# Turning x by small transfers and block transposes instead of by TensorE, in a fused attention and MLP kernel

## The chip, the core and the metric

The kernel runs on one core of one Trainium2 chip. The metric is device time in microseconds, from launch to the last output. The core has five engines that run side by side and wait for one another by semaphores: TensorE (PE in the profile, with its weight loads as PEld), VectorE (DVE), ScalarE (ACT), GpSimd (POOL) and SyncE (SP, which here only issues transfers). TensorE writes to PSUM, a memory of eight banks of 128 partitions x 512 floats; everything else lies in SBUF. Instructions of one engine run in the order in which the kernel writes them.

## What is computed

The reference, cut to what matters:

```
phi(x)[i,j] = (S1 x)[i] * (S2 x)[j]          # 8 x 8 = 64 features of a 32-wide row
kv  = sum over s of phi(k)[s] (x) v[s]       # 64 x 32 for each batch and head
z   = sum over s of phi(k)[s]                # 64
num = phi(q) kv ;  den = phi(q) z + 1e-6     # for each token and head
x   = num / den, the 4 heads side by side    # 4 x 1088 tokens, 128 wide
out = x + relu(layernorm(x) * g @ w1) @ w2   # 128 -> 512 -> 128
```

There are 4 batches, 4 heads, 1088 tokens and a head width of 32; all data are float32.

## The kernel before, in words

**Chunks.** The 4352 tokens are cut into nine chunks. Chunks 0 to 7 are 512 tokens each, two to a batch (four tiles of 128 tokens); chunk 8 (`LAST`) collects the last 64 tokens of all four batches in two tiles. For a chunk c these stages follow one another:

- `query_rows(c)` (L316): DVE turns the chunk's q by 32x32 blocks (L233; L325 for chunk 8), so that the head dimension lies on partitions.
- `query_features(c)` (L329): 32 matmuls (L340) put both factors of the features into banks 0 to 3. ACT copies one factor to SBUF (L348) and DVE multiplies the other one, straight from the banks, with it (L349, tile `qp`).
- `numerators(c)` (L354): 64 small matmuls (L370) of the features with `kvz`, the batch's kv and z, into banks 0 and 1. DVE takes the denominators (L377), inverts them (L382) and writes x = num / den (L384): tokens on partitions, 128 columns to a tile.
- `statistics(c)` (L394): DVE takes mean and variance of each tile (L401), and six small POOL instructions finish the variance.
- `root(c)` (L418): ACT takes the root (L422), DVE the reciprocal (L426), and four POOL instructions (L427 to L432) refine it to `rstd`.
- `turn_x(c)` (L434): TensorE transposes the tiles of x into bank 7 (L440) and ACT copies them to SBUF (L442, tile `xT`), so that the 128 columns of x lie on partitions.
- `hidden(c, j)` for j of 0 to 3 (L444): w1 times `xT` into bank 4 or 5 in turn (L449), then relu on ACT (L452, tile `hT`). Mean and scale are folded in: the mean into w1, `rstd` into the end.
- `second(c)` (L458): 16 matmuls with w2 into bank 6 (L462); `result(c)` (L467): DVE adds x to `rstd` times the bank (L473), and SP issues four transfers of 32 rows each to the output (L483).

**Keys.** A batch's keys need `key_rows` (DVE, L233 and L246), `key_tokens` (copies of v), `key_features(b, part, at)` (TensorE, L266, and an ACT copy, L271), `key_products` (POOL, L282) and `key_values(b, at, t0, t1)` (TensorE, L299), which sums kv and z over nine tiles of tokens in one bank, here bank 3, and copies them out by ACT (L307, L309). Batch 0 and the preparation of w1 and w2 stand ahead of the loop.

**Order.** The order on every engine is written out by hand (`manual_schedule`, and the loop at L552). In iteration c the loop issues the hidden layer of chunk c, `root(c)`, the numerators of chunk c + 1, in odd iterations the features and products of a coming batch's keys, the statistics of c + 1, `second(c)`, `turn_x(c + 1)`, `query_rows(c + 2)`, `result(c)` and `query_features(c + 2)`. In iterations 2 and 4 `key_values` runs in two halves, one inside the hidden layer (ahead of j = 2) and one behind `second`. In iteration 7 `turn_x(8)` stands inside `second(7)`; the hidden layer of chunk 8 follows in iteration 8.

**Transfers.** Each transfer that SP or ACT issues signals on one of eight semaphores, taken in turn, so the ninth waits for the first to have landed. The page's part on issues calls the time from issue to that signal "us to landing".

Of the kernel before, what the change touches and what calls it, by code (L numbers as in the profile page):

```python
# [15 lines left out]
def _ap(t: bass.AP, p0: int, np_: int, off: int, free):  # L16

    p = list(t.ap)[0]
    return bass.AP(
        t.tensor, t.offset + p0 * p[0] + off, [[p[0], np_]] + [list(d) for d in free]  # L20
    )
# [8 lines left out]
def kernel(  # L30
# [26 lines left out]

    nc = tc.nc  # L60
    P = 128
    B, H, S, D = q.shape
    R = S1.shape[0]
    DM = H * D
# [11 lines left out]

    consts = ctx.enter_context(tc.tile_pool(name="consts", bufs=1))
    work = ctx.enter_context(tc.tile_pool(name="work", bufs=2))
    small = ctx.enter_context(tc.tile_pool(name="small", bufs=3))
    ps = ctx.enter_context(tc.tile_pool(name="ps", bufs=1, space=bass.MemoryType.PSUM))  # L80
    ctx.enter_context(tc.manual_schedule())
    banks = ps.tile([P, 8 * 512], F32, name="banks")
# [1 line left out]
    def bank(i):  # L84
        return banks[:, 512 * i : 512 * (i + 1)]
# [225 lines left out]
                kvp[F * (1 - i) : F * (2 - i), 0 : 2 * D1],  # L311
            )

    qTs, qps, xs, rs, mvs, xTs, hTs = {}, {}, {}, {}, {}, {}, {}

    def query_rows(c):  # L316
        if c > LAST:
# [36 lines left out]
    def numerators(c):  # L354


        if c > LAST:
            return
        x = xs[c] = work.tile([P, 512], F32, tag="x", name="x", bufs=3)
        qp, n = qps.pop(c), ntiles(c) // 2  # L360
        step = 64 if c < LAST else 32
        for i in range(n):
            for h in range(H):
                for half in range(2):
                    rows = slice(F * half, F * half + F)
                    for u in range(0, P, step):
                        kvz = kvzs[CHUNKS[c][0] if c < LAST else u // 32]
                        t, o = 256 * h + P * i + u, W * i + D1 * h
                        z = D1 * (h // 2) + (0 if h % 2 == half else 2 * D1)
                        nc.tensor.matmul(  # L370
                            bank(half)[u : u + step, o : o + D1], qp[rows, t : t + step],
                            kvz[rows, z : z + D1], start=True, stop=True,
                        )
        den = small.tile([P, 4 * H], F32, tag="den", name="den")
        rden = small.tile([P, 4 * H], F32, tag="rden", name="rden")
        m = n * H
        nc.vector.tensor_scalar(  # L377
            out=_ap(den, 0, P, 0, [[m, 2], [1, m]]),
            in0=_ap(banks, 0, P, D, [[512, 2], [D1, m]]),
            scalar1=1e-6, scalar2=None, op0=ALU.add,  # L380
        )
        nc.vector.reciprocal(rden[:, 0 : 2 * m], den[:, 0 : 2 * m])  # L382
        for half in range(2):
            nc.vector.tensor_tensor(  # L384
                out=_ap(x, 0, P, D * m * half, [[D, m], [1, D]]),
                in0=_ap(banks, 0, P, 512 * half, [[D1, m], [1, D]]),
                in1=_ap(rden, 0, P, m * half, [[1, m], [0, D]]),
                op=ALU.mult,
            )

    def ntiles(c):
        return 4 if c < LAST else 2

    def statistics(c):  # L394

        if c > LAST:
            return
        n, x = ntiles(c), xs[c]
        st = small.tile([P, 4 * 6], F32, tag="st", name="st")
        for i in range(n):  # L400
            nc.vector.bn_stats(out=st[:, 6 * i : 6 * i + 6], in_=x[:, DM * i : DM * (i + 1)])  # L401
        d, s, va, r1 = (
            small.tile([P, 4], F32, tag=tag, name=tag)[:, 0:n] for tag in ("d", "s", "va", "r1")
        )

        def of(k):
            return _ap(st, 0, P, k, [[6, n]])

        tt, ts = nc.gpsimd.tensor_tensor, nc.gpsimd.tensor_scalar
        tt(out=d, in0=of(1), in1=of(4), op=ALU.subtract)  # L410
        tt(out=s, in0=of(2), in1=of(5), op=ALU.add)
        tt(out=d, in0=d, in1=d, op=ALU.mult)
        ts(out=s, in0=s, scalar1=1.0 / DM, scalar2=1e-6, op0=ALU.mult, op1=ALU.add)
        ts(out=d, in0=d, scalar1=0.25, scalar2=None, op0=ALU.mult)
        tt(out=va, in0=d, in1=s, op=ALU.add)
        mvs[c] = va, r1

    def root(c):  # L418

        n = ntiles(c)  # L420
        va, r1 = mvs.pop(c)
        nc.scalar.activation(r1, va, AF.Sqrt)  # L422
        r0 = small.tile([P, 4], F32, tag="r0", name="r0")[:, 0:n]
        rs[c] = small.tile([P, 4], F32, tag="rstd", name="rstd")
        tt = nc.gpsimd.tensor_tensor
        nc.vector.reciprocal(r0, r1)  # L426
        tt(out=r1, in0=va, in1=r0, op=ALU.mult)  # L427
        tt(out=r1, in0=r1, in1=r0, op=ALU.mult)
        nc.gpsimd.tensor_scalar(
            out=r1, in0=r1, scalar1=-0.5, scalar2=1.5, op0=ALU.mult, op1=ALU.add  # L430
        )
        tt(out=rs[c][:, 0:n], in0=r0, in1=r1, op=ALU.mult)  # L432

    def turn_x(c):  # L434
        if c > LAST:
            return
        n, x = ntiles(c), xs[c]
        xp = bank(7)
        for i in range(n):
            nc.tensor.transpose(xp[:, P * i : P * i + P], x[:, DM * i : DM * (i + 1)], ident)  # L440
        xT = xTs[c] = work.tile([P, 512], F32, tag="xT", name="xT")
        nc.scalar.copy(xT[:, 0 : P * n], xp[:, 0 : P * n])  # L442

    def hidden(c, j):  # L444
        n = P * ntiles(c)
# [7 lines left out]

    def second_at(c, i):

        return bank(6)[:, DM * i : DM * (i + 1)] if c < LAST else bank(6 + i)[:, 0:DM]

    def second(c, i0=0, i1=4):  # L458
        hT = hTs[c]
# [7 lines left out]
    def result(c):  # L467
        n = ntiles(c)
        ob = work.tile([P, 512], F32, tag="ob", name="ob", bufs=3)
        x, rstd = xs.pop(c), rs.pop(c)  # L470
        for i in range(n):
            t = slice(DM * i, DM * (i + 1))
            nc.vector.scalar_tensor_tensor(  # L473
                out=ob[:, t], in0=second_at(c, i), scalar=rstd[:, i : i + 1], in1=x[:, t],
                op0=ALU.mult, op1=ALU.add,
            )
        by_p0, by_part = steps(CHUNKS[c][0])
        for p0 in range(4):
            if c < LAST:
                row, eng = CHUNKS[c][0] * S + by_part * CHUNKS[c][1] + by_p0 * p0, nc.sync  # L480
            else:
                row, eng = p0 * S + 32, (nc.sync, nc.scalar)[p0 % 2]
            eng.dma_start(  # L483
                out=bass.AP(out.tensor, out.offset + row * DM, [[G * DM, 32], [1, n * DM]]),
                in_=ob[32 * p0 : 32 * p0 + 32, 0 : n * DM],
            )
# [5 lines left out]
    def first_weight(i):  # L492

        w1p, terms = bank((4, 7)[i]), w1_terms[i]
        for j, term in enumerate(terms):
            nc.tensor.matmul(  # L496
                w1p[:, 0:256], center, term, start=(j == 0), stop=(j == len(terms) - 1)
            )
        nc.scalar.copy(w1[:, 256 * i : 256 * i + 256], w1p[:, 0:256])
# [49 lines left out]
        nc.gpsimd.tensor_tensor(out=w2, in0=up, in1=rest[0], op=ALU.add)  # L549


    for c in range(LAST + 1):  # L552
        b = c // 2 + 1
        even = c > 0 and c % 2 == 0 and b < B
        if c == LAST:
            root(c)
        for j in range(JC):
            if (c, j) == (0, 1):
                first_weight(1)
            if j == 2 and even:  # L560
                key_values(b, 3, 0, 5)
            hidden(c, j)
        if c == 0:
            query_features(1)
            for part in range(3):
                key_features(1, part, (4, 7, 5)[part])
                key_products(1, part, nc.gpsimd)
            for part in range(3):
                key_tokens(1, part, nc.scalar)
            numerators(1)  # L570
            statistics(0)
            root(0)
            second(0)
            key_values(1, 3, 0, NT)
        else:
            if c < LAST:
                root(c)
            numerators(c + 1)
        if c % 2 == 1 and b + 1 < B:
            for part in range(3):  # L580
                key_features(b + 1, part, 2 + part % 2)
                key_products(b + 1, part, nc.gpsimd)
        statistics(c + 1)
        if c == LAST - 1:
            second(c, 0, 3)
            turn_x(LAST)
            second(c, 3, 4)
        elif c > 0:
            second(c)
        if even:  # L590
            key_values(b, 3, 5, NT)
        if c < LAST - 1:
            turn_x(c + 1)
        query_rows(c + 2)
        result(c)
        query_features(c + 2)
        if c % 2 == 0 and b + 1 < B:
            fill(b + 1)
            for part in range(3):
                key_tokens(b + 1, part, nc.gpsimd)  # L600
                key_rows(b + 1, part)


# [28 lines left out]
```

## Time and profile before

| what | value |
|---|---|
| time, median of 3 runs | 119.75 us (119.69 to 120.51) |
| span of the profiled execution | 121.6 us, mean granted clock 0.953 |
| TensorE busy | 111.2 us of the span, 91% |
| DVE, ACT, POOL busy | 59.0, 46.6, 39.1 us |
| share of TensorE in the chain that ended last | 82% |
| transposes of x (L440) | 34 matmuls, 5.9 us busy |
| copies of turned x (L442) | 9, 5.1 us on ACT |

The profiled execution took 123.42 us as a run. Its TensorE clock was granted at half rate between about 14 and 25 us of the span and at full rate afterwards, so what is read from 27 us on is read at full clock. How to read it: "busy" adds up instructions by engine; the chain of waits goes back from the last instruction to what released each step; an engine's row of digits has 40 slices of the span, in tenths.

### The profile page before, as it was taken

How to read it: one execution, taken by the hardware profiler on the slowest of the kernel's cores; microseconds unless marked ns; L12 is line 12 of the kernel's file. 1: busy time of each engine (PE TensorE's matmuls, PEld its weight loads, DVE VectorE, ACT ScalarE, POOL GpSimd, SP SyncE). 2: the span in 40 equal slices, each digit the busy share in tenths (PEclk: the TensorE clock that was granted, in tenths of full speed). 3: DMA queues.
4: the chain of work that ended last, by engine and by line, in shares of the span. 5: the costliest groups of instructions: out<-in, count | busy, mean ns of one | idle time of the engine just before them, and what ended most of it. 6: DMA issues, size and time to landing. Idle time of an engine off the chain costs nothing.

```text
span 121.6 us, 4288 instructions
## 1 busy us (share of the span) xinstructions
PE 111.2 (91%) x1833; PEld 80.3 (66%) x1833; DVE 59.0 (49%) x181; ACT 46.6 (38%) x109; POOL 39.1 (32%) x125
## 2 busy tenths in 40 slices
PE   5947877997999999999999999999999999999980
PEld 5826734536996399459845994598469549729770
DVE  1757679404644771616526825083417528414320
ACT  4145214259006740742176207403650570452420
POOL 4028000404967069402800892042014004204120
PEclk9999855599999999999999999999999999999997
DMA  2949999999402100210030003000300110030031
GB/s 63 306 102 309 325 211 314 225 304 258 146 3 65 29 5 3 52 40 5 0 86 5 0 5 85 7 0 5 86 0 5 41 45 5 3 89 5 0 86 43
DMA packets 8068, 10.24 MB, mean 84 GB/s; under 512 B 2417, under 2 KB 5617, under 8 KB 8049
## 3 DMA queue, kind: packets, MB, share of 16 engines
q1 hardware_dynamic: 7792, 9.38, 29.3%
q10 hardware_dynamic: 256, 0.59, 1.6%
q8 instruction: 14, 0.23, 0.8%
q14 instruction: 6, 0.04, 0.1%
HBM read 7.74 MB, written 2.23 MB: 82 GB/s over the span
## 4 chain that ended last, share of the span: by engine, by line
PE 82%; DMA 6%; DVE 3%; ACT 2%; SPq 2%; issue 1%; POOL 1%; ACTq 0%; POOLq 0%
PE banks L449 28%; PE banks L462 26%; PE banks L370 8%; PE banks L340 7%; PE banks L299 6%; PE banks L440 4%; DMA qn<-in_q_dram 4%; PE banks L266 2%; DMA vn<-in_v_dram 2%; PE banks L496 1%; DVE qp L349 1%; ACT xT L442 1%; SPq L105 1%; DVE x L384 1%; SPq L116 1%
## 5 line engine op out<-in xcount | busy, mean ns | idle before, releaser
L449 PE MATMUL banks<-xT,w 128*128 128x512 f32 (+1 forms) x72 | 35.1, 622 | 0.8 <-ACT xT L442 0.7
L462 PE MATMUL banks<-w,hT 128*128 128x128 f32 x272 | 32.9, 278 | 0.0
L462 PEld LDWEIGHTS banks<-w,hT 128*128 128x128 f32 x272 | 31.3, 192 | 0.4
L452 ACT ACTIVATE hT<-banks 128x512 f32<-128x512 f32 (+1 forms) x36 | 20.8, 576 | 13.4 <-PE banks L449 13.3
L449 PEld LDWEIGHTS banks<-xT,w 128*128 128x128 f32 x72 | 12.6, 200 | 16.7 <-ACT hT L452 7.1
L282 POOL TENSOR_TENSOR kp<-fs 128x1024 f32<-128x1024 f32 (+1 forms) x10 | 15.3, 1552 | 11.4 <-ACT fs L271 11.2
L349 DVE TENSOR_TENSOR qp<-banks,qb 128x512 f32<-128x512 f32 (+1 forms) x18 | 11.1, 656 | 15.0 <-ACT qb L348 15.0
L473 DVE SCALAR_TENSOR_TENSOR ob<-banks,rstd,x 128x128 f32<-128x128 f32 x34 | 9.7, 343 | 14.8 <-PE banks L462 6.9
L427 POOL TENSOR_TENSOR r<-va,r 128x4 f32<-128x4 f32 (+1 forms) x9 | 1.8, 201 | 45.0 <-DVE r L426 38.7
L370 PEld LDWEIGHTS banks<-kvz,qp 64*64 64x64 f32 (+1 forms) x576 | 9.0, 131 | 7.0 <-issue 3.8
L442 ACT COPY xT<-banks 128x512 f32<-128x512 f32 (+1 forms) x9 | 5.1, 563 | 22.0 <-PE banks L440 22.0
L370 PE MATMUL banks<-kvz,qp 64*64 64x33 f32 (+1 forms) x576 | 10.1, 219 | 1.3 <-DVE qp L349 0.9
L426 DVE RECIPROCAL r<-r 128x4 f32<-128x4 f32 (+1 forms) x9 | 1.6, 176 | 19.6 <-ACT r L422 19.6
L348 ACT COPY qb<-banks 128x512 f32<-128x512 f32 (+1 forms) x18 | 9.2, 566 | 4.1 <-PE banks L340 4.1
L299 PEld LDWEIGHTS banks<-v,kp 128*32 128x32 f32 (+3 forms) x432 | 7.7, 118 | 4.1 <-issue 3.1
L299 PE MATMUL banks<-v,kp 128*32 128x33 f32 (+3 forms) x432 | 8.6, 207 | 1.5 <-ACT qb L348 1.1
L340 PE MATMUL banks<-qT,wb 32*64 32x256 f32 (+1 forms) x144 | 6.7, 387 | 1.0 <-DVE qT L233 1.0
L401 DVE BATCH_NORM_STATS2 st<-x 128x6 f32<-128x128 f32 x34 | 7.3, 278 | 0.0
L384 DVE TENSOR_TENSOR x<-banks,rden 128x256 f32<-128x256 f32 (+1 forms) x18 | 6.5, 404 | 0.3
L440 PE MATMUL banks<-ident,x 128*128 128x128 f32 x34 | 5.9, 296 | 0.8 <-DVE sc L177 0.8
L340 PE MATMUL banks<-qT,wa 32*64 32x256 f32 (+1 forms) x144 | 6.3, 362 | 0.0
L233 DVE STREAM_TRANSPOSE qT<-qn 128x512 f32<-128x512 f32 x8 | 5.6, 699 | 1.4 <-DMA qn<-in_q_dram 1.4
(63 smaller groups left out, 91.4 us busy)
## 6 DMA issues: line engine op xcount, KB each, us to landing
out_dram<-ob SPq DMA_DIRECT2D x32, 64.0 KB, 1.7
kn<-in_k_dram SPq DMA_DIRECT2D x3, 544.0 KB, 6.1
qn<-in_q_dram SPq DMA_DIRECT2D x3, 544.0 KB, 5.6
vn<-in_v_dram SPq DMA_DIRECT2D x12, 128.0 KB, 5.9
vn<-in_v_dram SPq DMA_DIRECT2D x8, 64.0 KB, 3.2
w_raw<-in_moe_w_ch_dram ACTq DMA_DIRECT2D x1, 512.0 KB
w_raw<-in_moe_w_ch_dram SPq DMA_DIRECT2D x1, 512.0 KB
kn<-in_k_dram SPq DMA_DIRECT2D x1, 288.0 KB, 3.0
```

The lines of the kernel that those rows point to most:

```text
L282: eng.tensor_tensor(out=_ap(kp, 0, m, t0 * H * F, [[F, tiles * H], [R, R], [1, R]]), in0=_ap(kf, 0, m, 0, [[R2, tiles * H], [1, R], [0, R] ...
L299: nc.tensor.matmul(kvp[o : o + step, D1 * (h // 2) : D1 * (h // 2 + 1)], kp[0:m, H * F * t + f : H * F * t + f + step], v1[0:m, W * t + D1 ...
L340: nc.tensor.matmul(bank(h)[F * half : F * half + F, o : o + n], w[rows, :], qT[rows, n * half : n * half + n], start=True, stop=True,)
L348: nc.scalar.copy(own, _ap(banks, 0, P, 512 * h, [[512, 2], [1, n]]))
L349: nc.vector.tensor_tensor(out=_ap(p, 0, P, 256 * h, [[256, 2], [1, n]]), in0=_ap(banks, 0, P, 512 * h + 256, [[512, 2], [1, n]]), in1=own, ...
L370: nc.tensor.matmul(bank(half)[u : u + step, o : o + D1], qp[rows, t : t + step], kvz[rows, z : z + D1], start=True, stop=True,)
L384: nc.vector.tensor_tensor(out=_ap(x, 0, P, D * m * half, [[D, m], [1, D]]), in0=_ap(banks, 0, P, 512 * half, [[D1, m], [1, D]]), in1=_ap(r ...
L440: nc.tensor.transpose(xp[:, P * i : P * i + P], x[:, DM * i : DM * (i + 1)], ident)
L449: nc.tensor.matmul(hp[:, 0:n], w1[:, P * j : P * (j + 1)], xTs[c][:, 0:n], start=True, stop=True)
L452: nc.scalar.activation(hTs[c][:, 512 * j : 512 * j + n], hp[:, 0:n], AF.Relu)
L462: nc.tensor.matmul(second_at(c, i), hT[:, 512 * j + P * i : 512 * j + P * i + P], w2[:, DM * j : DM * (j + 1)], start=(j == 0), stop=(j == ...
L473: nc.vector.scalar_tensor_tensor(out=ob[:, t], in0=second_at(c, i), scalar=rstd[:, i : i + 1], in1=x[:, t], op0=ALU.mult, op1=ALU.add,)
```

## The change

From chunk 3 on, TensorE no longer turns x. A turned 128 x 128 tile is made of 32 x 32 blocks, each of them turned, with the blocks' places swapped across the diagonal. DVE can turn every block in place[...]. So `send_x` first moves the blocks by 16 small transfers on SP (32 partitions by 512 bytes each, 256 bytes for chunk 8), and `blocks_x` then turns all of them in one DVE instruction, which writes `xT` straight to SBUF: no bank and no ACT copy. For rows of a block to be contiguous, x of chunks 3 to 8 is laid out by head first (`x_steps`, `x_tile`).

A transfer takes time, so the order moves: the numerators of a chunk are now issued two iterations ahead of its hidden layer instead of one, the query features three ahead instead of two, the keys' values in bank 7 (bank 5 for batch 1) instead of bank 3, the first half of `key_values` at the end of the odd iteration, and the hidden layers of chunks 7 and 8 one behind the other. Iterations 0 and 1 are written out.

```diff
-    small = ctx.enter_context(tc.tile_pool(name="small", bufs=3))
+    small = ctx.enter_context(tc.tile_pool(name="small", bufs=4))
...
-        x = xs[c] = work.tile([P, 512], F32, tag="x", name="x", bufs=3)
+        x = xs[c] = work.tile([P, 512], F32, tag="x", name="x", bufs=4)
...
+    def x_steps(c):
+        return (DM, D) if c < 3 else (D, D * ntiles(c))
...
+    def send_x(c):
+        if c > LAST:
+            return
+        x, m = xs[c], D * ntiles(c)
+        xb = xbs[c] = work.tile([P, 512], F32, tag="xb", name="xb")
+        for p0 in range(4):
+            for h in range(H):
+                nc.sync.dma_start(
+                    out=xb[D * h : D * h + 32, m * p0 : m * p0 + m],
+                    in_=x[32 * p0 : 32 * p0 + 32, m * h : m * h + m],
+                )
+
+    def blocks_x(c):
+        if c > LAST:
+            return
+        n = ntiles(c)
+        xT = xTs[c] = work.tile([P, 512], F32, tag="xT", name="xT")
+        nc.vector.transpose(
+            _ap(xT, 0, P, 0, [[32, 4], [P, n], [1, 32]]),
+            _ap(xbs.pop(c), 0, P, 0, [[D * n, 4], [D, n], [1, D]]),
+        )
...
-        return bank(6)[:, DM * i : DM * (i + 1)] if c < LAST else bank(6 + i)[:, 0:DM]
+        return bank(6)[:, DM * i : DM * (i + 1)] if c < LAST else bank((7, 0)[i])[:, 0:DM]
...
+    mlp_in(0, {1: lambda: first_weight(1)})
+    query_features(1)
+    keys(1, (4, 7, 5))
+    for part in range(3):
+        key_tokens(1, part, nc.scalar)
+    numerators(1)
+    statistics(0)
+    root(0)
+    statistics(1)
+    second(0)
+    key_values(1, 5, 0, NT)
+    turn_x(1)
+    query_rows(2)
+    result(0)
+    query_features(2)
+    query_rows(3)
+    keys_in(2)
+
+    mlp_in(1, {2: lambda: query_features(3)})
+    root(1)
+    numerators(2)
+    keys(2, (2, 3, 7))
+    statistics(2)
+    numerators(3)
+    send_x(3)
+    statistics(3)
+    second(1)
+    turn_x(2)
+    query_rows(4)
+    result(1)
+    query_features(4)
+    key_values(2, 7, 0, 5)
+
+    for c in range(2, LAST + 1):
+
+        b = (c + 3) // 2
+        odd, some = c % 2 == 1, b < B
         if c == LAST - 1:
+            blocks_x(LAST)
+        if c < LAST:
+            mlp_in(c, {2: lambda: key_values(b, 7, 5, NT)} if some and not odd else {})
+        if c == LAST - 1:
+            mlp_in(LAST, {})
+        root(c)
+        numerators(c + 2)
+        send_x(c + 2)
         if c < LAST - 1:
+            blocks_x(c + 1)
+        if some and odd:
+            keys(b, (2, 3, 7))
+        statistics(c + 2)
+        second(c)
+        query_rows(c + 3)
         result(c)
+        query_features(c + 3)
+        if some and odd:
+            key_values(b, 7, 0, 5)
+        if b + 1 < B and not odd:
+            keys_in(b + 1)
```

Here `mlp_in(c, between)` issues the four `hidden(c, j)`, with what `between` names ahead of its j; `keys(b, at)` is the features and products of a batch's keys in the three banks named; `keys_in(b)` is its rows and tokens.

More of the change, by code (lines that the diff above doesn't have):

```diff
@@ L312, in key_values @@
             )
-    qTs, qps, xs, rs, mvs, xTs, hTs = {}, {}, {}, {}, {}, {}, {}
+    qTs, qps, xs, rs, mvs, xTs, hTs, xbs = {}, {}, {}, {}, {}, {}, {}, {}
     def query_rows(c):
@@ L383, in numerators, with x_tile @@
         for half in range(2):
+            by_i, by_h = x_steps(c)
             nc.vector.tensor_tensor(
-                out=_ap(x, 0, P, D * m * half, [[D, m], [1, D]]),
-                in0=_ap(banks, 0, P, 512 * half, [[D1, m], [1, D]]),
-                in1=_ap(rden, 0, P, m * half, [[1, m], [0, D]]),
+                out=_ap(x, 0, P, by_i * n * half, [[by_i, n], [by_h, H], [1, D]]),
+                in0=_ap(banks, 0, P, 512 * half, [[W, n], [D1, H], [1, D]]),
+                in1=_ap(rden, 0, P, m * half, [[H, n], [1, H], [0, D]]),
                 op=ALU.mult,
             )
+    def x_steps(c):
+        return (DM, D) if c < 3 else (D, D * ntiles(c))
+    def x_tile(c, i):
+        by_i, by_h = x_steps(c)
+        return _ap(xs[c], 0, P, by_i * i, [[by_h, H], [1, D]] if c >= 3 else [[1, DM]])
     def ntiles(c):
@@ L397, in statistics @@
             return
-        n, x = ntiles(c), xs[c]
+        n = ntiles(c)
         st = small.tile([P, 4 * 6], F32, tag="st", name="st")
         for i in range(n):
-            nc.vector.bn_stats(out=st[:, 6 * i : 6 * i + 6], in_=x[:, DM * i : DM * (i + 1)])
+            nc.vector.bn_stats(out=st[:, 6 * i : 6 * i + 6], in_=x_tile(c, i))
         d, s, va, r1 = (
@@ L436, in turn_x @@
             return
-        n, x = ntiles(c), xs[c]
+        n = ntiles(c)
         xp = bank(7)
         for i in range(n):
-            nc.tensor.transpose(xp[:, P * i : P * i + P], x[:, DM * i : DM * (i + 1)], ident)
+            nc.tensor.transpose(xp[:, P * i : P * i + P], x_tile(c, i), ident)
         xT = xTs[c] = work.tile([P, 512], F32, tag="xT", name="xT")
         nc.scalar.copy(xT[:, 0 : P * n], xp[:, 0 : P * n])
+    def send_x(c):
[12 more added lines that the diff above has]
+            return
+        n = ntiles(c)
+        xT = xTs[c] = work.tile([P, 512], F32, tag="xT", name="xT")
[3 more added lines that the diff above has]
+        )
     def hidden(c, j):
@@ L469, in result @@
         ob = work.tile([P, 512], F32, tag="ob", name="ob", bufs=3)
-        x, rstd = xs.pop(c), rs.pop(c)
+        rstd = rs.pop(c)
         for i in range(n):
@@ L473, in result @@
             nc.vector.scalar_tensor_tensor(
-                out=ob[:, t], in0=second_at(c, i), scalar=rstd[:, i : i + 1], in1=x[:, t],
+                out=ob[:, t], in0=second_at(c, i), scalar=rstd[:, i : i + 1], in1=x_tile(c, i),
                 op0=ALU.mult, op1=ALU.add,
@@ L549, with keys, keys_in, mlp_in @@
         nc.gpsimd.tensor_tensor(out=w2, in0=up, in1=rest[0], op=ALU.add)
[L552 to L556, printed above, removed]
+    def keys(b, at):
+        for part in range(3):
+            key_features(b, part, at[part])
+            key_products(b, part, nc.gpsimd)
+    def keys_in(b):
+        for part in range(3):
+            key_tokens(b, part, nc.gpsimd)
+            key_rows(b, part)
+    def mlp_in(c, between):
@@ L557 @@
         for j in range(JC):
[L558 to L561, printed above, removed]
+            if j in between:
+                between[j]()
             hidden(c, j)
[L563 to L583, printed above, removed]
-        if c == LAST - 1:
[L585 to L591, printed above, removed]
-        if c < LAST - 1:
-            turn_x(c + 1)
-        query_rows(c + 2)
@@ L595 @@
-        result(c)
[L596 to L601, printed above, removed]
+    mlp_in(0, {1: lambda: first_weight(1)})
+    query_features(1)
+    keys(1, (4, 7, 5))
+    for part in range(3):
+        key_tokens(1, part, nc.scalar)
[5 more added lines that the diff above has]
+    key_values(1, 5, 0, NT)
```

## The prediction

> **What bounds the kernel now.** I read the page first, then the chain of waits in order of time, then timelines of DVE, SP and POOL. TensorE is busy for 91% of the span; no other engine passes half:
>
> ```profile
> PE 111.2 (91%) x1833; PEld 80.3 (66%) x1833; DVE 59.0 (49%) x181; ACT 46.6 (38%) x109; POOL 39.1 (32%) x125
> ...
> PEclk9999855599999999999999999999999999999997
> ```
>
> The clock row sets apart about 10 us at half rate early in this execution. It ran 123.42 us where the timed runs have 119.75, so I take no duration from before 27 us; the changed stages lie behind it. The chain around chunk 4, and then at the end:
>
> ```profile
> 59.52 0.82 PE banks L299 x60
> 60.34 0.59 PE banks L440 x4
> 60.93 1.30 PE banks L340 x29
> 62.22 3.74 PE banks L449 x8
> ...
> 104.52 0.45 PE banks L440 x4
> ...
> 105.05 0.60 ACT xT L442
> 105.64 0.04 issue
> 105.69 3.80 PE banks L449 x8
> ...
> 113.05 0.22 PE banks L440 x2
> 113.27 0.89 PE banks L462 x8
> 114.16 0.87 PE banks L449 x4
> 115.03 0.04 issue
> 115.07 1.13 PE banks L449 x4
> 116.20 1.87 PE banks L462 x16
> ```
>
> From 27 us on the chain is TensorE without gaps, with one step by ACT (the copy of turned x ahead of hidden(7)). So TensorE time removed counts in full, and so does each new wait of TensorE. Two more views carry the working: DVE after numerators in an even iteration (hidden(2) ends at 54.68), and SP issuing one chunk's output.
>
> ```profile
> 56.31 0.76 DVE L384 TENSOR_TENSOR x<-banks,rden 128x256 f32<-128x256 f32 x2
> 56.99 0.86 DVE L401 BATCH_NORM_STATS2 st<-x 128x6 f32<-128x128 f32 x4
> 57.77 0.69 DVE L233 STREAM_TRANSPOSE qT<-qn 128x512 f32<-128x512 f32 x1
> ```
>
> ```profile
> 95.72 1.73 SPq L483 DMA_DIRECT2D out_dram<-ob  x4
> ```
>
> ```profile
> L483 SPq DMA_DIRECT2D out_dram<-ob x34: 314/422/952, 37.6 to 118.8; - x34
> ...
> DMA to landing us min/median/max: 1.5/1.7/2.2
> ```
>
> Four issues take 1.73 us: a first one of 0.31 and three of about 0.42, with gaps of (1.73 - 0.31 - 1.27) / 3 = 0.05. So in a row one issue costs SP **0.47 us**, though a transfer here has only 32 rows; a landing comes 1.5 to 1.7 us after an issue.
>
> **What the Trainium skill says.** "VectorE: DVE Perf Modes", section "The three transpose paths": DVE turns 32x32 blocks only, into SBUF, while TensorE turns a full tile into PSUM. The trace agrees in kind: 0.69 us for a 128x512 block transpose, against four TensorE transposes (0.44 us) and an ACT copy (0.59). "DMA: Bandwidth & Descriptors", "Rules for kernel authors": many small transfers should be coalesced, under 64 KB one pays mostly overhead. The trace agrees for issue (0.47 us whatever the rows), and disagrees with the section "Issuing engines are not separate DMA queues", by which initiating is usually small beside the transfer: here 0.47 beside 1.7. "TensorE: Matmul & The Clock Gate", Part 1: about 3.4 us without work can halve the clock, and the window is free-running. The row of clocks shows such a halving once; I use it for a rival only.
>
> **The change part by part.**
>
> *Removed from TensorE.* The transposes of chunks 3 to 8: 0.59 + 0.44 + 0.59 + 0.44 + 0.45 + 0.22 = 2.73. The 0.15 by which two of them are longer sits behind `key_values` and may be its tail, which stays; without it 2.43. `query_features` takes 1.27, 1.30 and 1.29 us in iterations 0, 2 and 4, where it must wait for the copies of kv out of bank 3, and 1.05 elsewhere; with kv in banks 5 and 7 that is 3 x 0.24 = 0.7. Ahead of hidden(7) the chain shows 0.72 between transpose and hidden, in which query_features(8) lies anyway, with half the columns and so about 0.55: 0.17. Hidden(8) takes 0.87 + 0.04 + 1.13 = 2.04 with waits for relu; eight matmuls of half the columns of 3.74 are 1.87: 0.17. Sum 3.5 (to 3.8). The ACT copies (6 x 0.59) weren't on the path but for that one.
>
> *Added on DVE.* Five block transposes of 0.69, one of 0.42 (an estimate between 0.69 for 512 columns and 0.20 for 64). In an even iteration DVE ends `qT` at 58.46 now and second(2) ends at 59.52, so with 0.7 more and some tens of ns for waits on up to eight semaphores it ends at 59.2 to 59.5: hidden, just. Since `query_features` now follows `second` directly, I allow 0.2 in all (0 to 0.9) over iterations 2, 4 and 5; in odd iterations with keys 1.42 us of key features cover it.
>
> *Iteration 1.* query_features(3) stands inside hidden(1), ahead of j = 2, so 1.91 us behind query_features(2). Its `qT` is queued on DVE behind the products of chunk 2. In the trace these products start 0.75 after query_features(2) ends (38.55) and end 2.04 after; with 0.69 for `qT`, TensorE waits until 2.70: **0.8**. After it two hidden steps (1.91) run before numerators(2) needs banks 0 and 1, which the products of chunk 3 free 2.1 behind query_features(3): 0.2 more; and 0.05 for splitting hidden. **1.05** (0.3 to 1.3). Numerators(3) needs x(2) out of the banks, 1.4 behind numerators(2); the keys between take 1.42.
>
> *Keys.* key_values(b, 7, 0, 5) needs two products, which in iteration 1 end 6.1 us after hidden (POOL starts 2.2 after, 1.95 each); TensorE arrives 1.07 + 1.42 + 3.77 + 1.05 = 7.3 after. Nothing. kv is copied out behind two hidden steps, 1.9 us against 0.65 of ACT: nothing.
>
> *Transfers, steady.* 16 + 4 issues x 0.47 = 9.4 us of SP per iteration; iterations last 9.6 to 12.8 us. x(c + 2) is ready 2.4 after hidden(c) ends, its sends are issued until 9.9, the output of chunk c until 11.8; the last send lands by 11.1, and blocks_x wants it 2.4 into the next iteration, 11.5 to 15 after: hidden.
>
> *Transfers, the end.* This pays. Count from the end of hidden(5). x(7) is ready at 2.4; 16 sends occupy SP to 9.9; result(5), issued behind them, to 11.8; only then can the 16 sends of chunk 8 go, though x(8) is ready at 10.9. The last is issued at 11.8 + 15 x 0.47 = 18.9, lands at 20.5, and the block transpose ends at 21.0. TensorE gets to hidden(8) after numerators(7) 1.07, second(5) 3.77, query_features(8) 0.55, hidden(6) 3.73, numerators(8) 0.69, second(6) 3.77 and hidden(7) 3.74: at 17.3. It waits **3.7 us**, and second(7) and second(8) are queued behind the waiting matmul. Bounds: at 0.31 an issue 0.5; at 0.52, one stumble like the 0.95 in the row above per batch, 4.7.
>
> *The last root.* root(8)'s reciprocal stands on DVE behind result(7). Now hidden(8) lies between that and second(8):
>
> ```profile
> 115.53 0.20 POOL L427 TENSOR_TENSOR r<-va,r 128x2 f32<-128x2 f32 x1 [2.47 <-DVE r L426]
> ...
> 116.37 0.19 POOL L432 TENSOR_TENSOR rstd<-r,r 128x2 f32<-128x2 f32 x1
> ```
>
> `rstd` is ready at 116.56, 2.40 after second(7) ended (114.16). Afterwards only second(8), 1.87, follows second(7): `rstd` comes 0.53 too late, and both result instructions run behind it, where now one is done early (0.3): **0.85**.
>
> Sum: 119.75 - 3.5 + 1.05 + 0.2 + 3.7 + 0.85 = **122.0**.
>
> **Rivals.**
> 1. *The transfers stay hidden.* If SP issues these short transfers at 0.31, the tail wait is 0.5 or nothing, and the order pays: 119.75 - 3.5 + 1.05 + 0.2 + 0.85 = 118.4, or 117.5 without the wait for `rstd`. For it: 0.31 is seen, for the first of a row. Against: every longer row shows 0.42 and more.
> 2. *Half the tail wait.* At about 0.40 with gaps the sum of issues shrinks by 36 x 0.07 = 2.5 and the wait to 1.3: 119.6, no change.
> 3. *Worse.* A pause of 3.7 us can halve the clock; one window of 3.4 us at half rate costs 1.7, so 123.7. Or DVE, held by late sends, holds query_features in several iterations, 0.5 to 1 each: 123 to 124. Against it: the steady count leaves 0.4 us or more.
>
> **How the numbers follow.** The forecast gets 0.52, rival 1 0.15, rival 2 0.20, rival 3 0.13. The two bounds of the tail wait alone reach from 118.8 to 123.0; with rival 3 in part, 118.7 to 123.5 leaves out most of rival 1 and the end of rival 3, two in ten. Faster by over 1% (under 118.55): 0.14. Within 1%: rival 2 and the short end of the forecast, 0.22. Slower (over 120.95): 0.64.
>
> **What would show it.** Right, if TensorE idles 3 to 4 us ahead of hidden(8), released by the block transpose and that by a landing; if SP's rows of 16 sends take about 7.5 us; if query_features(3) waits 0.8 us for `qT`; if the last result waits for `rstd`; and if no L440 is left after chunk 2. Wrong, if a send costs clearly less than 0.4 us of SP, or if TensorE waits for block transposes in iterations 2 to 6.

## The result, and the profile after

The changed kernel takes 141.97 us where the kernel before, measured beside it, takes 120.13: ratio **1.171** (1.159 to 1.183), 19 to 22 us slower. The forecast was slower, at 122.0; the direction held, the size is off by a factor of about ten. Single runs of one kernel differ by some us, the longer ones with a lower granted TensorE clock; each ratio and its interval leave the longer runs out, a median without a ratio does not, so small differences below are read from ratios or from the traces.

The page of the changed kernel, the parts that answer to those shown of before: busy time, granted clock, the chain by engine, and the issues of sends.

```profile
PE 113.5 (79%) x1811; PEld 80.9 (56%) x1811; DVE 62.4 (43%) x187; ACT 43.5 (30%) x103; POOL 39.0 (27%) x125
...
PEclk9999555999999999999999599999986999755899
...
PE 38%; SPq 31%; issue 11%; DVE 9%; DMA 4%; ACT 2%; POOL 2%; DVEq 0%; POOLq 0%
...
xb<-x SPq DMA_DIRECT2D x80, 16.0 KB, 1.8
```

TensorE fell from 91% to 79% of a longer span. In the chain, where it had 82%, it has 38%, and SP's issues, which were no part of the chain behind the loads, have 31%. The clock row has new dips besides the early one. By the trace's clock record it stands at half rate from 79.3 to 82.7, from 106.6 to 110.0 and from 123.7 to 133.9 us. Each of these stretches begins inside one of the three longest pauses of TensorE (2.35, 3.34 and 7.79 us, below) or at most 1.5 us behind it; behind the pauses of 1.60, 0.78 and 2.04 us there is none. That the pauses cause the dips is not tested apart.

The view of the tile that the sends write, and the chain of waits of the changed kernel towards its end:

```profile
L463 SPq DMA_DIRECT2D xb<-x x96: 512/589/1794, 49.2 to 126.7; - x96
```

```profile
113.10 0.59 SPq L463
113.73 0.59 SPq L463
114.32 0.05 issue
114.42 2.45 DMA out_dram<-ob
...
125.47 0.59 SPq L463
126.11 0.59 SPq L463
126.74 1.79 DMA xb<-x
...
128.71 0.46 DVE xT L473
129.16 0.14 issue
129.30 3.75 PE banks L483 x8
```

A send occupies SP for 0.589 us and the next starts 0.04 to 0.05 later: **0.63** against the 0.47 of the prediction. From the first send, at 49.2 us, to the end of the last, at 127.3, SP issues without a break: sixteen sends, the four transfers of an output, sixteen sends, and so on, as a queue that never runs empty. TensorE at hidden(8) (L483) waits for the block transpose, that for the last landing, that for SP.

How the wait reaches TensorE in the other iterations is seen in the timeline of DVE around the block transpose of chunk 4 (iteration 3), in TensorE's timeline at the query features behind it and at hidden(7) and hidden(8), and in the sums of waits (us in total, times, longest):

```profile
76.24 0.71 DVE L473 STREAM_TRANSPOSE xT<-xb 128x512 f32<-128x512 f32 x1 [3.86 <-DMA xb<-x]
76.88 0.83 DVE L412 BATCH_NORM_STATS2 st<-x 128x6 f32<-128x128 f32 x4
77.62 0.69 DVE L235 STREAM_TRANSPOSE qT<-qn 128x512 f32<-128x512 f32 x1
```

```profile
78.37 0.69 PE L342 MATMUL banks<-qT,wb 32*64 32x256 f32 x16 [2.35 <-DVE qT L235]
...
117.65 3.86 PE L483 MATMUL banks<-xT,w 128*128 128x512 f32 x8 [2.04 <-DVE xT L473]
129.30 3.75 PE L483 MATMUL banks<-xT,w 128*128 128x256 f32 x8 [7.79 <-DVE xT L473]
```

```profile
PE banks L483 <- DVE xT L473: 9.8, 2, 7.8
PE banks L342 <- DVE qT L235: 6.6, 5, 2.4
PE banks L342 <- DVE qT L327: 3.3, 1, 3.3
```

DVE stands for 3.86 us at a block transpose whose blocks have not landed. Behind it in its queue are the statistics and the turned q of a later chunk, and for that q TensorE waits 2.35 us, though the x that the block transpose turns is needed only later. At hidden(7) and hidden(8) it waits for x itself, 2.04 and 7.79 us. The two profiled spans differ by 22.0 us: TensorE is busy 2.3 us longer and idle 19.7 us longer. Of the idle time 17.9 us are waits behind late blocks, from iteration 2 on: 9.8 for `xT` and 8.1 for `qT` (1.60, 2.35, 0.78 and 3.34). The other 1.9 us of waits for `qT` are not due to the sends: 0.87 lies in iteration 1 and comes with the new order, 1.0 lies in the loading part and is there before as well. That busy time grew, although work was taken from TensorE, comes from matmuls at half rate behind the pauses (hidden(8) takes 3.75 us where 1.87 were due).

### The profile page after: what moved, and what is told of

The parts are those of the page before. It is cut to its first block, busy times and chain, and to the rows that moved or that the text cites. A ratio compares the mean times of both kernels' runs of the same rounds, so it can differ in the third digit from the quotient of the medians.

```text
span 143.6 us, 4359 instructions
## 1 busy us (share of the span) xinstructions
PE 113.5 (79%) x1811; PEld 80.9 (56%) x1811; DVE 62.4 (43%) x187; ACT 43.5 (30%) x103; POOL 39.0 (27%) x125
## 4 chain that ended last, share of the span: by engine, by line
PE 38%; SPq 31%; issue 11%; DVE 9%; DMA 4%; ACT 2%; POOL 2%; DVEq 0%; POOLq 0%
SPq L463 27%; PE banks L483 13%; PE banks L496 8%; PE banks L301 5%; PE banks L372 5%; PE banks L342 4%; SPq L517 4%; DVE qp L351 3%; DMA xb<-x 3%; DMA out_dram<-ob 2%; PE banks L451 2%; DVE x L387 1%; ACT qb L350 1%; PE banks L530 1%; DVE qT L235 1%
## 5 line engine op out<-in xcount | busy, mean ns | idle before, releaser
L483 PE MATMUL banks<-xT,w 128*128 128x512 f32 (+1 forms) x72 | 39.6, 691 | 10.5 <-DVE xT L473 9.8
L483 PEld LDWEIGHTS banks<-xT,w 128*128 128x128 f32 x72 | 14.8, 228 | 27.7 <-issue 16.3
L473 DVE STREAM_TRANSPOSE xT<-xb 128x512 f32<-128x512 f32 (+1 forms) x6 | 4.0, 667 | 24.3 <-DMA xb<-x 18.4
L342 PE MATMUL banks<-qT,wb 32*64 32x256 f32 (+1 forms) x144 | 6.0, 387 | 9.9 <-DVE qT L235 6.6
L301 PE MATMUL banks<-v,kp 128*32 128x33 f32 (+3 forms) x432 | 9.1, 216 | 1.4 <-ACT qb L350 1.1
L342 PEld LDWEIGHTS banks<-qT,wb 32*64 32x64 f32 x144 | 2.2, 129 | 12.7 <-DVE qT L235 5.3
L421 POOL TENSOR_TENSOR d<-st 128x4 f32<-128x4 f32 (+1 forms) x9 | 1.8, 201 | 18.4 <-DVE st L412 18.4
```

The source lines that it names most:

```text
L301: nc.tensor.matmul(kvp[o : o + step, D1 * (h // 2) : D1 * (h // 2 + 1)], kp[0:m, H * F * t + f : H * F * t + f + step], v1[0:m, W * t + D1 ...
L342: nc.tensor.matmul(bank(h)[F * half : F * half + F, o : o + n], w[rows, :], qT[rows, n * half : n * half + n], start=True, stop=True,)
L483: nc.tensor.matmul(hp[:, 0:n], w1[:, P * j : P * (j + 1)], xTs[c][:, 0:n], start=True, stop=True)
```

## Experiments

Theory S: SP's time for issuing sends is the limit. Rivals: the new order costs the time (O); a send's price is per row or byte (R); the landings and DVE's waits in order set the time whatever the number of sends (L); the DMA engines are the limit (D).

**The order alone.** `send_x` is empty, `blocks_x` calls `turn_x`, x stays in the layout of before:

```diff
     def x_steps(c):
 
-        return (DM, D) if c < 3 else (D, D * ntiles(c))
+        return DM, D
...
     def blocks_x(c):
         if c > LAST:
             return
...
-        nc.vector.transpose(
-            _ap(xT, 0, P, 0, [[32, 4], [P, n], [1, 32]]),
-            _ap(xbs.pop(c), 0, P, 0, [[D * n, 4], [D, n], [1, D]]),
-        )
+        turn_x(c)
```

> Part of the change alone: the new order of the work and the new banks, but x of all chunks is turned by TensorE in bank 7 (at the place of the block transpose), with no sends. Theory S (the rate at which SP issues the 96 sends sets the time): without sends the 20 us are gone; by the prediction's own terms 119.75 - 0.7 (bank 3) - 0.3 (tail of TensorE) + 1.05 (iteration 1) + 0.85 (last root) + 0.2 = about 121, and TensorE has no wait over 1.2 us after 45 us. Rival O (the new order itself costs it: numerators two ahead, banks 2, 3 and 7, in-order waits on DVE): stays above 130.

Measured: 120.98 (119.98 to 122.67) beside 120.65 (118.18 to 124.31) for the kernel before, medians of 4 and 7 runs. The 20 us are gone, so rival O falls. A cost of a us or two could not be told in so few runs; with two places mended, the new order comes out at a ratio of 1.001 below. The chain of waits in iteration 1 has the first wait that the prediction priced there:

```profile
33.01 1.13 PE banks L342 x32
...
36.07 0.63 DVE qT L235
36.70 0.14 issue
36.84 1.19 PE banks L342 x32
```

query_features(2) ends at 34.14 and query_features(3) begins at 36.84, 2.70 later, just as worked out.

**Fewer, wider sends.** The same bytes in 8 sends of 64 partitions, or 4 of 128 (blocks at wrong places):

```diff
-        for p0 in range(4):
+        for p0 in range(2):
             for h in range(H):
                 nc.sync.dma_start(
-                    out=xb[D * h : D * h + 32, m * p0 : m * p0 + m],
-                    in_=x[32 * p0 : 32 * p0 + 32, m * h : m * h + m],
+                    out=xb[64 * p0 : 64 * p0 + 64, m * h : m * h + m],
+                    in_=x[64 * p0 : 64 * p0 + 64, m * h : m * h + m],
                 )
```

> The changed kernel with 8 sends per chunk of 64 partitions in place of 16 of 32; the same bytes reach xb, but the blocks lie at wrong places, so the output is not the reference's. Theory S, with a price per instruction: 8 x 0.63 + 4 x 0.47 = 6.9 us of SP per chunk, under the 9.6 us of the shortest iteration, so DVE no longer waits for transfers and the time falls to 118 to 120. Rival R (a send's price is per row or per byte): 64 rows cost SP twice as much, nothing changes, about 140. Rival L (the way there and back, landing plus the in-order wait on DVE, sets the time whatever the number): over 130.

> As the run with 64 partitions, with 4 sends of 128 partitions per chunk: the same bytes, blocks at wrong places. Theory S: 4 x 0.63 + 1.9 = 4.4 us of SP per chunk, no wait of hidden(8) for a transfer, 118 to 119, at most 0.5 less than with 8 sends. Rival R: about 140. Rival L: over 130.

Measured: 122.43 (119.99 to 123.73) with 8 sends and 118.62 (117.74 to 121.63) with 4, beside 120.65 for the kernel before. The tile views of the two:

```profile
L463 SPq DMA_DIRECT2D xb<-x x48: 467/595/1737, 47.0 to 104.9; - x48
```

```profile
L463 SPq DMA_DIRECT2D xb<-x x24: 470/599/1799, 48.7 to 104.0; - x24
```

A send of 64 or 128 rows costs SP what one of 32 rows costs (0.595 and 0.599 us against 0.589), so rival R falls, and D with it: the DMA engines move the same bytes in the same rows, and 20 us are gone. L falls because the number of sends decides: the way through the landing and DVE's waits in order is the same. 118 to 120 was expected with 8 sends; three of its four runs lie 1.6 to 3.7 us above that. In the trace TensorE waits once for a block transpose, at hidden(8), for 1.52 us: x(8) is there at 99.7, eight sends with one of 1.43 us among them take until 104.9, the landing 1.84, and hidden(7) ends at 106.0. I had counted from the end of SP's queue alone and 0.3 of wait. The rest of the distance is not assigned.

**What an issue costs.** The kernel before, with eight idle transfers behind each of five outputs:

```diff
         result(c)
+        if 2 <= c <= 6:
+            price(c)
         query_features(c + 2)
```

> The kernel before with eight idle transfers behind the output of each of chunks 2 to 6, for what an issue costs SP: chunk 2 SBUF to SBUF, 32 rows of 512 bytes, from other partitions; chunk 3 the same within the same partitions; chunk 4 SBUF to SBUF, 128 rows of 512 bytes; chunk 5 from HBM to SBUF, 32 rows of 512 bytes; chunk 6 SBUF to SBUF, 32 rows of 128 bytes. Theory B (both ends in SBUF is what costs): about 0.59 us in chunks 2, 3, 4 and 6 and 0.43 in chunk 5. Rival P (moving to other partitions costs): 0.59 in chunk 2 alone. Rival N (short runs cost): 0.59 in chunks 2 to 5, more in 6. Rival Q (a full queue holds SP): under 0.5 for the first sends of each row, more for the later ones.

The views of the tiles that they write, one line for each of chunks 2 to 6 in this order:

```profile
L412 SPq DMA_DIRECT2D scratch<-kn x8: 583/590/953, 62.5 to 67.3; - x8
...
L412 SPq DMA_DIRECT2D scratch<-kn x8: 512/590/1174, 75.2 to 80.1; - x8
...
L412 SPq DMA_DIRECT2D scratch<-kn x8: 538/600/1588, 87.0 to 91.4; - x8
...
L412 SPq DMA_DIRECT2D scratch<-in_q_dram x8: 419/420/425, 97.5 to 100.8; - x8
...
L412 SPq DMA_DIRECT2D scratch<-kn x8: 561/589/1376, 107.6 to 112.8; - x8
```

Theory B stands: 0.59 to 0.60 us in the median with both ends in SBUF, whether the rows change partitions or not, with 32 or 128 rows, with 512 or 128 bytes; 0.42 from HBM with the very shape of a send. Rivals P and N fall with that. Q falls because no issue inside SBUF, the first of a row or a later one, is under 0.51.

**The prediction's price put back.** 15 of the 16 sends read HBM instead of x, so xb does not hold x:

```diff
-                nc.sync.dma_start(
-                    out=xb[D * h : D * h + 32, m * p0 : m * p0 + m],
-                    in_=x[32 * p0 : 32 * p0 + 32, m * h : m * h + m],
-                )
+                if (p0, h) == (0, 0):
+                    i = x[0:32, 0:m]
+                else:
+                    i = bass.AP(q.tensor, q.offset + 512 * (4 * p0 + h), [[G * D, 32], [1, m]])
+                nc.sync.dma_start(out=xb[D * h : D * h + 32, m * p0 : m * p0 + m], in_=i)
```

> The changed kernel with the price of a send alone put back to what the prediction assumed: still 16 sends of 32 rows x 512 bytes, but 15 of them read from HBM (from q) instead of from x; the first still reads x, so that SP waits for x as before. The blocks in xb are not x, so the output is not the reference's. The run of prices has 0.42 + 0.04 us for such an issue. Theory S: SP has 16 x 0.47 + 1.9 = 9.4 us per chunk and the prediction's own sum applies: about 122, with 3 to 4 us of TensorE idle ahead of hidden(8). Rival L (the number of transfers or the way over SBUF as such costs, not SP's time for an issue): stays above 130.

Measured: 127.88, ratio 1.061 (1.049 to 1.073). The price is worth about 14 of the 20 us, but 122 was not reached.

```profile
L467 SPq DMA_DIRECT2D xb<-in_q_dram x90: 311/420/1942, 46.5 to 110.3; - x90
```

```profile
104.22 3.86 PE L484 MATMUL banks<-xT,w 128*128 128x512 f32 x8 [1.68 <-DVE xT L474]
112.81 3.63 PE L484 MATMUL banks<-xT,w 128*128 128x256 f32 x8 [4.74 <-DVE xT L474]
```

At 0.42 SP still issues without a break from 45.9 to 110.7. The 96 sends and 20 output transfers of this stretch, at 0.465 with the gap, are 53.9 of its 64.8 us; nine long issues, "stumbles" below, of 0.87 to 1.94 us, add 8.7 to that. From the first send of a chunk to that of the next SP needs 11.4 us in the mean, not 9.4, and that is over the 9.6 of the short iterations. The wait at hidden(8), put at 3.7 for this price, is 4.74, and hidden(7) waits too. So the stumbles are a second term that was too small, apart from the price; this is read from the sum of one trace, and no run takes them away.

**Half of the sends on ACT.**

```diff
-                nc.sync.dma_start(
+                (nc.sync, nc.scalar)[h % 2].dma_start(
```

> The changed kernel with every second send issued by ACT in place of SP; nothing else. Theory S (SP's time for issues, not the DMA engines, is the limit): SP has 8 x 0.63 + 1.9 = 6.9 us per chunk and no longer limits; ACT gets 8 x 0.6 = 5 us per chunk more, between relus, so TensorE waits for ACT: 121 to 130, clearly under 138. Rival D (the DMA engines or the landings limit): no gain, about 140.

Measured: 144.35, ratio 1.195 (1.179 to 1.211): no faster than with all sends on SP, where theory S expected 121 to 130. The chain of waits, ACT's issues and what is queued behind them:

```profile
105.58 0.52 ACTq L463
106.10 0.04 issue
106.14 0.86 ACTq L463
...
111.05 0.60 ACTq L463
...
112.40 0.51 ACT hT L486
112.91 0.04 issue
112.95 2.51 PE banks L483 x4
```

Eight issues hold ACT from 105.58 to 111.65, and before that it stood waiting for x; copies and relus queue behind, and TensorE behind these. The limit has moved from SP to ACT; what eight issues in a row do to the relus behind them was priced too low. The run can't tell S from D, since both have a reason for its time; the wide sends do that.

**By way of HBM.** Four writes of 32 rows and one read of 128, in the place of 16 sends:

```diff
+        turn = nc.dram_tensor(f"turn{c}", [P, 512], F32).ap()
         for p0 in range(4):
-            for h in range(H):
-                nc.sync.dma_start(
-                    out=xb[D * h : D * h + 32, m * p0 : m * p0 + m],
-                    in_=x[32 * p0 : 32 * p0 + 32, m * h : m * h + m],
-                )
+            nc.sync.dma_start(
+                out=bass.AP(turn.tensor, turn.offset + m * p0, [[512, 32], [32 * 512, H], [1, m]]),
+                in_=_ap(x, 32 * p0, 32, 0, [[m, H], [1, m]]),
+            )
+        nc.sync.dma_start(out=xb[:, 0 : 4 * m], in_=turn[:, 0 : 4 * m])
```

> The changed kernel with the blocks moved by way of HBM: four writes of 32 rows x 4 pieces of 512 bytes, then one read of 128 rows, five issues at HBM prices in place of 16. Theory S: SP has 5 x 0.47 + 1.9 plus about 1.7 us of waiting for the writes to land, 6 us per chunk; no wait of hidden(8) beyond 0.5: the prediction's sum without the tail wait, 118 to 119. Rival L: the two landings in a row come too late for the block transpose and DVE holds TensorE: over 121.

Measured: 119.35, ratio 0.986 (0.972 to 1.000). By that ratio it would be 118.1 where the kernel before is at 119.75, near the prediction's sum without the tail wait, 118.4; the interval, 116.4 to 119.8, is too wide to test the terms of that sum. A short tail wait is left: TensorE stands 0.75 us ahead of hidden(8).

**The two places of the order.**

```diff
-        root(c)
+        if c < LAST:
+            root(c)
+        if c == LAST - 1:
+            root(LAST)
...
     query_rows(2)
+    query_rows(3)
     result(0)
     query_features(2)
-    query_rows(3)
```

> As the run over HBM, with two places of the order mended: the root of chunk 8 ahead of second(7), which the prediction priced at 0.85, and query_rows(3) ahead of result(0), priced at 0.8. If both terms are right, 1.6 us less than the run over HBM, about 116.8; if they were never on the path, no difference.

> The version over HBM with the root of chunk 8 ahead of second(7), but query_rows(3) where the change has it. The prediction priced that place at 0.8: about 0.8 slower than with both places mended, and TensorE waits about 0.8 us for qT of chunk 3 in iteration 1. If DVE's order there isn't on the path, no difference.

> The version over HBM with both places mended, a second time and in more rounds, beside the two others: 117 to 118, 2 to 3% under the kernel before.

Measured: both places, 0.980 (0.969 to 0.990) in the first comparison and **0.979** (0.970 to 0.988) in the second; the root alone, 0.979 (0.971 to 0.988). The last lines of the chain, without the mended root and with both places:

```profile
111.95 4.27 PE banks L497 x39
116.22 0.52 DVE ob L508 x2
...
117.45 0.19 POOL r L440
...
117.95 0.35 DVE ob L508
```

```profile
105.58 5.37 PE banks L497 x48
110.95 0.02 issue
110.97 0.35 DVE ob L508
```

Without it, the 48 matmuls that take 5.37 us end at 117.32 and the last result at 118.30, 0.98 later; with it 0.37 later. By these chains the root's place cost 0.6; the ratios, 0.986 and 0.980, overlap. Of query_rows(3) the ratios show nothing, 0.979 with and without it, but their intervals reach about 1 us to either side and can't exclude the 0.8 expected. The traces can. The chains in iteration 1, query_features(2) and the start of second(1), first with the root alone mended and then with both places:

```profile
34.59 1.13 PE banks L342 x32
...
45.22 0.86 PE banks L497 x6
```

```profile
32.89 1.13 PE banks L342 x32
...
42.82 3.21 PE banks L497 x27
```

From the end of query_features(2) to second(1) it is 9.50 us with the old place and 8.80 with the new one. The distance between the two query features falls from 2.69 to 1.98 us, where it ends because the banks must be freed next. The 0.7 us last to the end: from the end of query_features(2) to the last matmul TensorE's timeline has 78.0 and 78.1 us in the two runs over HBM with the old place, 77.4 and 77.0 in the two with the new one.

**Is the turning itself worth it?** The same two places mended, but all x turned by TensorE and no transfers:

> The new order with all x turned by TensorE and no sends (as in order_alone), plus the two mended places: root of chunk 8 ahead of second(7), query_rows(3) ahead of result(0). Theory S: turning x on DVE is worth the TensorE time of the six transposes, so this is 2 to 3 us slower than the version over HBM with the same two places: about 119.5 when that one is at 117.5. Rival: the transposes were hidden and the whole gain is the order: the two are within 0.5 us.

Measured: ratio 1.001 (0.996 to 1.005), against 0.979 (0.970 to 0.988) for the version over HBM beside it. The difference of 2.2% is 2.6 us, give or take 1.2. In the traces the stretch from the end of query_features(2) to the last matmul is 78.9 us here, 1.4 to 1.9 longer than over HBM, where 0.6 to 0.7 of wait ahead of hidden(8) is still in it. So turning by DVE is worth about what the prediction put on the transposes themselves, 2.4 to 2.7. The rival falls.

## Why the prediction was wrong

- **What bounds the kernel**: right for before. It said that a new wait of TensorE counts in full, and the span grew by TensorE's new idle time, 19.7 us, and 2.3 us of busy time.
- **Removed from TensorE, 3.5 us**: right in its main term. 1.4 to 2.6 us, by traces and by ratio, lie between turning by DVE and by TensorE in an otherwise equal kernel. The 0.7 for bank 3 is nearly there too: in the new order the query features that took 1.30 us in iterations 2 and 4 take 1.05.
- **Added on DVE, 0.2**: over HBM TensorE has no wait above 0.1 us from iteration 2 on to hidden(8), so the block transposes as such cost it nothing there.
- **Iteration 1, 1.05**: right. The first wait is in the trace as worked out (2.70 after query_features(2), and in `order_alone` numerators(2) follow query_features(3) by 1.98, against 2.1; TensorE waits 0.86 and 0.14 us), and moving query_rows(3) takes 0.7 us out of the path.
- **Keys in bank 7, nothing**: nothing of it is among the waits of TensorE.
- **The last root, 0.85**: right in kind, 0.6 in size.
- **"Transfers, steady": this step failed.** It priced a send at 0.47 us by the output rows of SP, "though a transfer here has only 32 rows", took that as a price for any shape, and found 9.4 us of SP per chunk beside iterations of 9.6 to 12.8: "hidden". The row that I took has HBM at one end; a send has SBUF at both, and costs 0.63. The sum becomes 16 x 0.63 + 4 x 0.47 = 12.0, and the stumbles (nine in the trace, 7.2 us over the medians of their kinds in all) add 1.2 per chunk. That is above the iterations, so SP is the bound from the first send on: 96 sends x 0.633 + 20 output transfers x 0.47 + 7.2 = 77.4 us, where the trace has 78.2 from the first send at 49.2 to the end of the last at 127.3. Put at nothing, this term cost TensorE 10.1 us of waits ahead of hidden(8).
- **"Transfers, the end", 3.7 us**: the same two terms. The count of 36 issues started from an idle SP at x(7); in the trace the queue runs without a break from the sends of chunk 3 on, and the wait at hidden(8) is 7.79 us. The direction of the forecast rests on this term, which was right in kind; most of the loss came from the one above.
- **The bounds**: 0.31 to 0.52 for an issue was drawn from spread within one kind of transfer. No row of before has both ends in SBUF, so the range had to hold another kind, and a stumble per chunk, of which the trace had one of 0.95 in 34. Rival 3 named the mechanism (DVE, held by late sends, holds query_features; the clock falls in a pause) and gave it 123 to 124, too near, because it kept 0.4 us of slack per chunk that does not exist. Two of the new stretches at half rate last 3.4 us, as it had it, the last one 10.2.
- **Rival 1**, 118.4 with hidden transfers, is near what the kernel does once there are few transfers: 118.1 by way of HBM, where 0.75 us of tail wait is left.

## What to carry to other kernels

A serial queue that issues transfers is an engine like the others: multiply issues by their price and hold the sum, with a share for stumbles, against the shortest iteration; near it, a fixed excess per iteration adds up to the end instead of staying hidden. Price an operation from a row of the same kind at both ends, and where there is none, let the range say so. A block move that needs many small transfers inside SBUF can be cheaper by way of HBM, where one transfer carries more pieces. Put the waiting instruction behind what other engines need, since an engine in order passes its wait on. One way was not tried: to move the blocks by instructions of ACT or DVE. The copies of kv on ACT (L309 of the kernel before, 0.21 us each) read one half of the partitions and write the other.

## What was not expected of the hardware

An issue with both ends in SBUF takes 0.59 us on SP, 0.42 with one end in HBM, whatever the rows, bytes and partitions that were tried. On ACT an issue with both ends in SBUF took 0.61 us in the median, 0.52 to 1.67. Single issues take 0.9 to 1.9 us. In the changed kernel and in the one with the price put back, nine 16 KB packets of a queue that loads instructions fall into the stretch in which SP issues without a break, and the nine long issues stand at them one to one, starting at most 0.7 us apart. That these loads cause them is not tested. The time to landing does not follow this split: its median is 1.8 us both for a send inside SBUF and for a write to HBM (up to 4.0 for sends, next to long issues), and 2.8 for the read of 128 rows behind the writes, by the view of the tile that this read fills, in the version over HBM with both places mended:

```profile
DMA to landing us min/median/max: 2.6/2.8/2.9
```
